# Numerators and weight sums of a plain pair of heads in one 128-row matmul, in the gate stages of a fused attention and GEGLU kernel

## The chip, the cores and the metric

One core of one Trainium2 chip. The metric is the device time of one execution in microseconds (us), the median of several; the executions of one kernel in one comparison lie 0.5 to 2.3 us apart. Ratios are the mean time of one kernel's runs over the mean of the other's runs of the same rounds, so they are not quite the ratio of the medians that are quoted.

## The reference

Attention over 8 batches, 8 heads, 576 positions and 64 dimensions, with a window of 32 keys; heads 0 to 3 ("plain") look at adjacent keys, heads 4 to 7 ("dilated") at every fourth. The heads' outputs, side by side, are 4608 tokens of 512 and go through a GEGLU block.

```python
scores = scale * np.matmul(q, k.transpose(0, 1, 3, 2))
mask_plain = (rel >= 0) & (rel < window)
mask_dil = (rel >= 0) & (rel < window * dilation) & (rel % dilation == 0)
...
attn = np.exp(scores)
attn = attn / (np.sum(attn, axis=-1, keepdims=True) + 1e-09)
out = np.matmul(attn, v)
...
g = x @ w_gate
gelu = 0.5 * g * (1.0 + erf(g * inv_sqrt2))
return gelu * (x @ w_val) @ w_out
```

## The kernel before

It works through 9 chunks of 512 tokens. A chunk has a gate stage (12 units of eight 512-column matmuls: four for the gate, four for the values of the GEGLU, then a gelu on ScalarE and a multiply on VectorE) and an output stage. The attention of later batches is slotted between these matmuls, two heads ("a pair") at a time: 32 pairs, four to a batch, the first two of each batch plain. This study is about seven plain pairs that fall into the gate stages of chunks 3 to 6: 16, 20, 21, 24, 25, 28 and 29.

The kernel's matmuls write to PSUM, which it uses as eight banks of 512 columns. The traces show a weight load for each matmul (2400 of each in the profile before; 98 ns long in the mean for a full one of L481): the operand loaded so is called stationary here. The other one is streamed, and the time goes with its columns: from one start to the next 0.216 us for 512.

For such a pair the kernel computes numerators (probabilities times values) and sums of weights (probabilities times ones), in 64-column tiles: head 0 to PSUM partitions 0 to 63 and head 1 to 64 to 127, at the same columns:

```python
# emit_pv, plain pairs, wide form (cuts marked ...)
for j in range(5):
    for hl in range(2):
        lhs = vp[:, j, 2 * hp + hl, :] if j < 4 else vt[:, 2 * hp + hl, :]
        w = (PW, PW, PW, P, PT)[j]                    # 160, 160, 160, 128, 64
        add(hl, j * P, run(w), lhs, ...)
...
groups = ((0, 0, 4, P), (P, P, 3, 32), (PH - PT, 512, 1, PT))   # 512, 96 and 64 columns
for i, (p0, q0, runs, w) in enumerate(groups):
    for hl in range(2):
        add(hl, d0 + q0, [[P, runs], [1, w]], ones[:, 0:D], ...)
```

VectorE then turns the sums into factors and multiplies. The transpose is used in 18 blocks of 32 columns, to bring the 576 sums, which lie along the columns, onto the partitions; the reciprocal is then taken of 18 columns only, and a second transpose spreads the result (0.78, 0.27 and 0.78 us in the trace before, from 266.04):

```python
# norm_r
nc.vector.transpose(dst, den)                          # 128 x 576, from PSUM
nc.vector.reciprocal(rc, dt[:, :, 0:1]...)             # 128 x 18
nc.vector.transpose(rb..., rc spread by a zero step)   # 128 x 576
# norm_x
nc.vector.tensor_tensor(dst, psf[:, b0 * 512 : b0 * 512 + S], rb, ALU.mult)
```

The gate stage's loop. The pair's four PSUM banks (SB and up) are free for the next pair when its product has been taken; a unit uses one of two pairs of banks in turn:

```python
for nb in range(NNB):                       # 12 units
    ...
    ffn1(c, nb, pairs[(nb + swap) % 2])     # 8 matmuls, then gelu and multiply
    if pend is not None:
        norm_x(pend, SB)
        pend = None
    if nb in pv_at:                         # values_a: chunk -> {unit: pair}
        pend = pv_at[nb]
        emit_pv(pend, SB, wide=True)
        norm_r(pend, SB, wide=True)
```

The softmax here doesn't subtract the row's maximum and nothing guards it: scores larger than these inputs give would overflow.

## Time and profile before

363.44 us, the median of three runs (363.22 to 364.12). The profile's span is 362.5 us, at a granted clock of 0.995.

| engine | busy us | share |
|---|---|---|
| TensorE (PE) | 345.5 | 95% |
| TensorE weight loads (PEld) | 164.2 | 45% |
| VectorE (DVE) | 184.8 | 51% |
| ScalarE (ACT) | 146.0 | 40% |
| GpSimd (POOL) | 78.2 | 22% |

How to read the lines in this document. A group of instructions has line, engine, operation, output <- input and shape, then busy us, the mean ns of one, idle us before it and what ended that idle time. A line of the timeline or of the chain of waits has start us, length us, engine and what ran, with "x8" for eight of it merged. In the chain, a q after an engine's name is its sequencer, and "issue" is time in which the engine waited for nothing that the profile shows. The end of a matmul is modelled, so two matmuls are compared by their starts. L481, L512 and L433 are, before, the gate stage's matmuls, the output stage's, and those of values and sums; after the change the same are L533, L564 and, for the seven changed pairs, L455 (L442 where the old form stays).

### The profile page before, as it was taken

The page shows a single profiled execution, that of the slowest core. Times are in us where ns is not written, and L with a number is a line of the kernel's source. Part 1 is how long each engine was busy: PE and PEld are TensorE (multiplying, and loading weights), DVE is VectorE, ACT ScalarE, POOL GpSimd, SP SyncE. Part 2 cuts the span into 40 slices and gives each one's busy share as a digit, 9 for nine tenths or more (in the row PEclk, how much of TensorE's full clock was granted, in tenths as well). Part 3 has the DMA queues.
Part 4 walks back from the last instruction along what each step waited for, and adds up shares of the span by engine and source line. Part 5 has one row for each costly group of instructions (what it writes and reads, how often), then busy time and mean ns, then how long its engine had stood idle before and what let it go on. Part 6 is the DMA issues. An engine that isn't in the chain of part 4 may idle for free.

```text
span 362.5 us, 6061 instructions
## 1 busy us (share of the span) xinstructions
PE 345.5 (95%) x2400; PEld 164.2 (45%) x2400; DVE 184.8 (51%) x278; ACT 146.0 (40%) x212; POOL 78.2 (22%) x110
## 2 busy tenths in 40 slices
PE   7879899999989999899999999999999999999995
PEld 2554354444544445444444444444444444444442
DVE  1585445744266325864477638783669413303320
ACT  1733255253543345434553356336542223312321
POOL 2580333540432332063003410240000000000000
PEclk9899999999999999999999999999999999999999
DMA  7999999999899898599438962893100030011002
GB/s 184 244 177 214 220 133 194 192 157 235 188 142 204 181 161 154 136 173 135 101 93 186 158 96 89 195 140 72 60 30 2 0 116 2 1 60 58 0 29 89
DMA packets 107292, 45.31 MB, mean 125 GB/s; under 512 B 83040, under 2 KB 102496, under 8 KB 107264
## 3 DMA queue, kind: packets, MB, share of 16 engines
q1 hardware_dynamic: 84272, 31.21, 39.8%
q0 software_dynamic: 21456, 12.01, 26.6%
q10 hardware_dynamic: 1536, 1.70, 2.0%
q8 instruction: 19, 0.31, 0.4%
q14 instruction: 9, 0.07, 0.1%
HBM read 40.13 MB, written 9.44 MB: 137 GB/s over the span
## 4 chain that ended last, share of the span: by engine, by line
PE 78%; DMA 13%; DVE 5%; POOL 2%; ACT 1%; issue 1%; ACTq 0%; SPq 0%; POOLq 0%; DVEq 0%
PE ps L481 41%; PE ps L512 25%; PE ps L433 5%; DMA xT<-in_k_dram 4%; DMA st<-in_k_dram 3%; PE ps L493 3%; DMA wv<-in_moe_w_val_dram 3%; DMA wo<-in_moe_w_out_dram 2%; DVE xT L469 2%; PE ps L360 1%; DMA sv<-in_v_dram 1%; PE ps L330 1%; DVE dt L451 1%; DVE rb L455 1%; PE ps L346 1%; POOL qp L251 1%
## 5 line engine op out<-in xcount | busy, mean ns | idle before, releaser
L506 DVE SCALAR_TENSOR_TENSOR u_all<-g,ps 128x512 f16<-128x512 f16 x108 | 73.5, 686 | 85.9 <-PE ps L481 76.9
L505 ACT ACTIVATE g<-ps 128x512 f16<-128x512 f32 x108 | 63.6, 597 | 126.0 <-PE ps L481 115.0
L512 PE MATMUL ps<-wo,u_all 128*128 128x512 f16 x432 | 101.1, 380 | 1.1 <-DMA wo<-in_moe_w_out_dram 0.7
L481 PE MATMUL ps<-xT,wg 128*128 128x512 f16 x392 | 100.7, 379 | 0.3
L481 PE MATMUL ps<-xT,wv 128*128 128x512 f16 x392 | 100.6, 379 | 0.0
L512 PEld LDWEIGHTS <-u_all 128*128 128x128 f16 x432 | 39.2, 98 | 45.4 <-issue 1.5
L481 PEld LDWEIGHTS <-wv 128*128 128x128 f16 x392 | 38.4, 98 | 46.4 <-issue 0.2
L481 PEld LDWEIGHTS <-wg 128*128 128x128 f16 x392 | 37.2, 98 | 45.0 <-issue 2.1
L523 ACT ACTIVATE osb<-ps 128x512 f32<-128x512 f32 x33 | 19.7, 597 | 49.0 <-PE ps L512 49.0
L451 DVE STREAM_TRANSPOSE dt<-ps 128x576 f32<-128x576 f32 x32 | 24.9, 779 | 26.2 <-PE ps L433 25.9
L190 POOL CAST qp<-st 128x2048 f16<-128x2048 f32 x6 | 11.4, 1894 | 99.0 <-DMA st<-in_k_dram 84.8
L455 DVE STREAM_TRANSPOSE rb<-rc 128x576 f32<-128x576 f32 x32 | 24.9, 778 | 1.1
L362 ACT ACTIVATE P<-ps 128x1152 f16<-128x1152 f32 x16 | 18.1, 1130 | 10.8 <-PE ps L360 10.8
L340 ACT ACTIVATE P<-ps 128x960 f16<-128x960 f32 x16 | 15.5, 970 | 10.7 <-PE ps L330 10.6
L469 DVE TENSOR_TENSOR xT<-ps,rb 128x576 f16<-128x576 f32 x16 | 17.9, 1126 | 0.3
L493 PE MATMUL ps<-xT,wg 128*128 128x512 f16 x40 | 15.2, 379 | 2.1 <-DVE xT L469 1.6
L525 DVE TENSOR_SCALAR osb<-ps 128x512 f32<-128x512 f32 x3 | 2.1, 691 | 28.8 <-PE ps L512 28.8
L433 PE MATMUL ps<-P,ones 128*64 128x96 f16 (+5 forms) x216 | 14.3, 245 | 1.6 <-ACT P L362 1.6
L493 PE MATMUL ps<-xT,wv 128*128 128x512 f16 x40 | 15.2, 379 | 0.0
L466 DVE TENSOR_TENSOR xT<-ps,rb 128x576 f16<-128x576 f32 x16 | 11.8, 745 | 0.3
L370 DVE TENSOR_TENSOR P<-P,mask_p 128x1344 f16<-128x1344 f16 x10 | 8.4, 852 | 6.8 <-ACT P L341 6.8
L370 DVE TENSOR_TENSOR P<-P,mask_d 128x1152 f16<-128x1152 f16 x8 | 6.1, 757 | 11.1 <-ACT P L362 11.1
(75 smaller groups left out, 244.2 us busy)
## 6 DMA issues: line engine op xcount, KB each, us to landing
out_dram<-osb SPq DMA_DIRECT2D x36, 256.0 KB, 2.1
sv<-in_v_dram SPq DMA_DIRECT2D x40, 128.0 KB, 3.2
st<-in_q_dram SPq DMA_DIRECT2D x24, 128.0 KB, 3.7
st<-in_k_dram SPq DMA_DIRECT2D x24, 128.0 KB, 3.1
qd<-in_q_dram POOLq DMA_DIRECT2D x7, 256.0 KB, 5.0
qd<-in_k_dram POOLq DMA_DIRECT2D x7, 256.0 KB, 6.9
vd<-in_v_dram POOLq DMA_DIRECT2D x7, 256.0 KB, 7.2
wg<-in_moe_w_gate_dram POOLq DMA_DIRECT2D x3, 512.0 KB, 7.4
```

Of the source, the lines that this page charges most:

```text
L340: nc.scalar.activation(pt[:, :, 0:PB], sb[:, 0, :, 0:PB], AF.Exp, bias=0.0, scale=scale)
L362: nc.scalar.activation(pt, ps[:, b0 : b0 + 4, 0:DW], AF.Exp, bias=0.0, scale=scale)
L433: nc.tensor.matmul(o, lhs, rhs, start=st, stop=True, skip_group_check=True)
L451: nc.vector.transpose(dst, den)
L455: nc.vector.transpose(rb.rearrange("p (b c) -> p b c", c=32), bass.AP(tensor=rc.tensor, offset=rc.offset, ap=[rc.ap[0], [1, 18], [0, 32]]),)
L469: nc.vector.tensor_tensor(dst.rearrange("p (i m s) -> p i m s", m=2, s=2), num, rb.rearrange("p (s m i) -> p i m s", s=2, m=2), ALU.mult,)
L481: nc.tensor.matmul(ps[:, b0 + gi, :], w[:, kc, ns], xT[kc][:, tok], start=(kc == 0), stop=(kc == NKC - 1))
L493: nc.tensor.matmul(ps[:, pairs[nb] + gi, :], w[:, kc, ns], xT[kc][:, tok], start=(kc == 0), stop=(kc == NKC - 1),)
L505: nc.scalar.activation(g, ps[:, b0, :], AF.Gelu)
L506: nc.vector.scalar_tensor_tensor(u_all[:, nb, :], g, USCALE, ps[:, b0 + 1, :], ALU.mult, ALU.mult)
L512: nc.tensor.matmul(ps[:, bank, :], u_all[:, fc, tb * P : (tb + 1) * P], wo_t[fc // 4][:, fc % 4, :], start=(fc == 0), stop=(fc == NNB - 1),)
L523: nc.scalar.activation(osb, ps[:, bank, :], AF.Copy, bias=0.0, scale=1.0 / USCALE)
```

## The change

The intent: put a head's values next to a block of ones in the stationary operand, so that one matmul of 128 columns gives the numerators of the head in 64 PSUM rows and its sums in the other 64. For the second head of a pair the same block of ones serves from the other side (values, ones, values), so its rows are swapped. The ten matmuls of a pair replace sixteen. Since numerators and sums of the two heads no longer share columns, VectorE needs two transposes and two products of 64 partitions each. The values get permanent tiles with the ones set at the start, the casts into them are strided, and the pairs of chunks 4 to 6 move to other units.

```diff
+    vset = [
+        (
+            const.tile([P, 4, HP, 3, D], F16, tag=f"vp{i}", name=f"vp{i}"),
...
+        nc.gpsimd.tensor_copy(
+            vp.rearrange("p j g x d -> p (j g) x d")[:, :, 0:3:2, :],
+            sv[:, 0:4].rearrange("p j (g x) d -> p (j g) x d", x=2),
+        )
...
+    def emit_both(n, b0):
...
+        for hl in range(2):
+            for j in range(5):
+                w = (PW, PW, PW, P, PT)[j]
+                p0 = j * PW - (32 if j == 4 else 0)
+                trio = vp[:, j, hp] if j < 4 else vt[:, hp]
+                nc.tensor.matmul(
+                    ps[:, b0 + 2 * hl + j // 4, j % 4 * P : j % 4 * P + w],
+                    trio[:, hl : hl + 2, :].rearrange("p x d -> p (x d)"),
+                    pt[:, hl, p0 : p0 + w],
+                    start=j in (0, 4),
+                    stop=True,
+                    skip_group_check=True,
+                )
+
+    def both_rows(half, b0, hl):
+        return psf[64 * half : 64 * half + 64, (b0 + 2 * hl) * 512 : (b0 + 2 * hl) * 512 + S]
+
+    def norm_both_r(n, b0):
+        dt = nrm.tile([P, 18, 32], F32, tag="dt", bufs=1)
+        for hl in range(2):
+            nc.vector.transpose(
+                dt[64 * hl : 64 * hl + 64].rearrange("p b c -> p (b c)"), both_rows(1 - hl, b0, hl)
+            )
+        recip(n, dt)
+
+    def norm_both_x(n, b0):
+        b, hp = divmod(n, NHP)
+        rb = tiles.pop(("rb", n))
+        for hl in range(2):
+            half = slice(64 * hl, 64 * hl + 64)
+            nc.vector.tensor_tensor(
+                xT[hp][half, b * S : (b + 1) * S], both_rows(hl, b0, hl), rb[half], ALU.mult
+            )
...
+    for vp_, _, vt_, _ in vset:
+        nc.vector.memset(vp_.rearrange("p j g x d -> p (j g) x d")[:, :, 1, :], 1.0)
+        nc.vector.memset(vt_[:, :, 1, :], 1.0)
...
-    values_a = {3: {4: 16}, 4: {3: 20, 6: 21}, 5: {2: 24, 4: 25, 6: 26}, 6: {1: 28, 3: 29, 5: 30, 7: 31}}
+    values_a = {3: {4: 16}, 4: {2: 20, 6: 21}, 5: {1: 24, 4: 25, 7: 26}, 6: {1: 28, 4: 29, 7: 30, 10: 31}}
...
-                norm_x(pend, SB)
+                (norm_both_x if is_plain(pend) else norm_x)(pend, SB)
...
+                if is_plain(pend):
+                    emit_both(pend, SB)
+                    norm_both_r(pend, SB)
+                else:
+                    emit_pv(pend, SB, wide=True)
+                    norm_r(pend, SB, wide=True)
```

More of the change, by code (lines that the diff above doesn't have):

```diff
@@ L80 @@
     ldp = ctx.enter_context(tc.tile_pool(name="ldp", bufs=1))
-    vpl = ctx.enter_context(tc.tile_pool(name="vpl", bufs=3))
     qtp = ctx.enter_context(tc.tile_pool(name="qtp", bufs=2))
@@ L100 @@
     xT = [const.tile([P, NT], F16, tag=f"xT{i}", name=f"xT{i}") for i in range(NKC)]
+    HP = HK // 2
+    vset = [
+        (
+            const.tile([P, 4, HP, 3, D], F16, tag=f"vp{i}", name=f"vp{i}"),
+            const.tile([P, HK, 4, D], F16, tag=f"vd{i}", name=f"vd{i}"),
+            const.tile([P, HP, 3, D], F16, tag=f"vt{i}", name=f"vt{i}"),
+            const.tile([P, HK, 2, D], F16, tag=f"vr{i}", name=f"vr{i}"),
+        )
+        for i in range(3)
+    ]
     u_all = const.tile([P, NNB, CH], F16, tag="u")
@@ L160, in new_v @@
     def new_v(b):
-        vp = vpl.tile([P, 4, HK, D], F16, tag="vp", name=f"vp{b}")
-        vd = vpl.tile([P, HK, 4, D], F16, tag="vd", name=f"vd{b}")
-        vt = vpl.tile([P, HK, D], F16, tag="vt", name=f"vt{b}")
-        vr = vpl.tile([P, HK, 2, D], F16, tag="vr", name=f"vr{b}")
         sv = ldp.tile([P, 5, HK, D], F32, tag="sv", name=f"sv{b}")
-        tiles["v", b] = (vp, vd, vt, vr)
+        tiles["v", b] = vset[b % 3]
         return sv
@@ L176, in v_cast @@
         vp, vd, vt, vr = tiles["v", b]
-        nc.gpsimd.tensor_copy(vp, sv[:, 0:4])
-        nc.gpsimd.tensor_copy(vt, sv[:, 4])
+        nc.gpsimd.tensor_copy(
+            vp.rearrange("p j g x d -> p (j g) x d")[:, :, 0:3:2, :],
+            sv[:, 0:4].rearrange("p j (g x) d -> p (j g) x d", x=2),
+        )
+        nc.gpsimd.tensor_copy(vt[:, :, 0:3:2, :], sv[:, 4].rearrange("p (g x) d -> p g x d", x=2))
     def load_qk_plain(b):
@@ L395, in emit_pv @@
                     for hl in range(2):
-                        lhs = vp[:, j, 2 * hp + hl, :] if j < 4 else vt[:, 2 * hp + hl, :]
+                        lhs = vp[:, j, hp, 2 * hl, :] if j < 4 else vt[:, hp, 2 * hl, :]
                         w = (PW, PW, PW, P, PT)[j]
@@ L433, in emit_pv @@
             nc.tensor.matmul(o, lhs, rhs, start=st, stop=True, skip_group_check=True)
+    def emit_both(n, b0):
+        b, hp = n // NHP, n % 2
+        pt = tiles["P", n]
+        vp, _, vt, _ = tiles["v", b]
+        for hl in range(2):
[27 more added lines that the diff above has]
+                xT[hp][half, b * S : (b + 1) * S], both_rows(hl, b0, hl), rb[half], ALU.mult
+            )
     def den_ap(n, b0, wide):
@@ L451, in norm_r, with recip @@
         nc.vector.transpose(dst, den)
+        recip(n, dt)
+    def recip(n, dt):
         rc = nrm.tile([P, 18], F32, tag="rc")
@@ L660 @@
                 pend = pv_at[nb]
-                emit_pv(pend, SB, wide=True)
-                norm_r(pend, SB, wide=True)
+                if is_plain(pend):
[4 more added lines that the diff above has]
+                    norm_r(pend, SB, wide=True)
             if c == 0 and nb in (9, 10):
```

## The prediction

> **What bounds the kernel now**
>
> I read, in this order, the page's summary and slices, its table of groups, the chain that ended last, and then the timeline of TensorE and of VectorE inside the stages that the change touches.
>
> The page first:
>
> ```profile
> span 362.5 us, 6061 instructions
> PE 345.5 (95%) x2400; PEld 164.2 (45%) x2400; DVE 184.8 (51%) x278; ACT 146.0 (40%) x212; POOL 78.2 (22%) x110
> PE 78%; DMA 13%; DVE 5%; POOL 2%; ACT 1%; issue 1%; ACTq 0%; SPq 0%; POOLq 0%; DVEq 0%
> L451 DVE STREAM_TRANSPOSE dt<-ps 128x576 f32<-128x576 f32 x32 | 24.9, 779 | 26.2 <-PE ps L433 25.9
> L466 DVE TENSOR_TENSOR xT<-ps,rb 128x576 f16<-128x576 f32 x16 | 11.8, 745 | 0.3
> ```
>
> TensorE (PE) is busy for 95% and the chain is 78% PE; from about 54 us on, the chain is PE nearly without a break. So the end moves by what PE issues, plus PE's rare waits. VectorE (DVE) averages 51%, but an average hides what it does inside one gate stage. The two DVE rows are the instructions that the change doubles for seven pairs.
>
> The gate stages concerned are chunks 3 to 6. In the chain of waits, chunk 6 (L481: gate and value matmuls; L433: values and sums of one pair):
>
> ```profile
> 260.98 0.86 PE ps L512 x4
> 261.84 3.45 PE ps L481 x16
> 265.29 0.70 PE ps L433 x16
> 266.00 3.56 PE ps L481 x16
> 269.55 0.70 PE ps L433 x16
> 270.26 3.57 PE ps L481 x16
> ...
> 278.25 0.72 PE ps L433 x12
> 278.97 7.01 PE ps L481 x32
> 285.98 10.36 PE ps L512 x48
> ```
>
> Each plain pair is a bite of PE time between two units of eight 512-column matmuls. In a later stage without pairs the chain has 96 such matmuls in 20.72 us: 0.216 us each, 1.727 us a unit. Chunks 3, 4, 5 and 6 last 18.24, 19.16, 23.20 and 24.14 us.
>
> What a bite really costs is in the PE timeline at the pair of chunk 3:
>
> ```profile
> 158.41 0.38 PE L481 MATMUL ps<-xT,wv 128*128 128x512 f16 x1
> 158.72 0.45 PE L433 MATMUL ps<-P,vp 128*64 128x160 f16 x8
> 159.01 0.20 PE L433 MATMUL ps<-P,vt 128*64 128x64 f16 x2
> 159.04 0.46 PE L433 MATMUL ps<-P,ones 128*64 128x512 f16 x6
> 159.43 0.61 PE L481 MATMUL ps<-xT,wg 128*128 128x512 f16 x2
> ```
>
> The last 512-column matmul starts at 158.41; the next start would be due 0.216 later, at 158.63, but is at 158.72: 0.09 lost on entering 64-column tiles. The next gate matmul starts at 159.43. So the bite is 159.43 - 158.63 = 0.80 us. The 16 matmuls run in pairs, two heads side by side, so they stream 672 columns of values and 672 of ones, 1344 column times in all.
>
> DVE's time of chunk 6:
>
> ```profile
> 266.04 0.78 DVE L451 STREAM_TRANSPOSE dt<-ps 128x576 f32<-128x576 f32 x1
> 266.85 0.27 DVE L453 RECIPROCAL rc<-dt 128x18 f32<-128x18 f32 x1
> 267.15 0.78 DVE L455 STREAM_TRANSPOSE rb<-rc 128x576 f32<-128x576 f32 x1
> 267.94 0.69 DVE L506 SCALAR_TENSOR_TENSOR u_all<-g,ps 128x512 f16<-128x512 f16 x1
> 268.54 0.75 DVE L466 TENSOR_TENSOR xT<-ps,rb 128x576 f16<-128x576 f32 x1
> ```
>
> Start to start a pair takes about 0.82 + 0.30 + 0.78 + 0.75 = 2.65 us of DVE, plus 0.6 to 0.69 for each unit's multiply. With a pair every two units (before) that is 3.9 us against 2 x 1.727 + 0.80 = 4.25 us of PE: DVE is nearly full here. Yet PE waits only twice in chunk 6: 0.06 us at 273.80 and 0.24 at 278.25.
>
> [...] 12 transposes of 128 columns take 0.84 us from first start to last end, each 0.22 long, so (0.84 - 0.22)/11 = 0.056 us apart. The weight load of 128 columns keeps up at that size.
> [...]
>
> **The change part by part**
>
> *PE, per plain pair in a gate stage.* Six matmuls over ones vanish (42 in all), ten of 64 columns become ten of 128, unpaired. Two heads x (3 of 160, one of 128, one of 64 columns) is again 1344 column times: the streaming is not reduced. What goes is the mode switch in and out and the starting cost. At 0.069, 0.056 and 0.029 us the new bite is 2 x (3 x 0.069 + 0.056 + 0.029) = 0.584 us. The old one is 0.80, plus 0.01 since the second gap after it is 0.227 and not 0.216. Saved: 0.81 - 0.585 = 0.22 us; seven pairs (16, 20, 21, 24, 25, 28, 29) make 1.55 us. All on PE, so on the path.
>
> *DVE, per such pair.* One transpose of the sums becomes two over 64 partitions, one product becomes two. Time follows the 576 columns, not the partitions, so I take 0.78 and 0.745 again for each half: +1.52 us[...]. Seven pairs: +10.7 us busy, off the path unless PE waits.
>
> *DVE at the start.* Six memsets: 3 x (0.48 + 0.15) = 2 us, right after the memset of ones at 0.9 us. DVE then idles 6.9 us for data, so nothing is lost.
>
> *POOL.* The value casts write strided runs of 64. 1024 elements now take 1.04 to 1.13 us (one contended one 1.60); a cast already in runs of 64 takes 0.82 for 768, the same rate. The first cast (18.84) lies on the startup chain, so 0.1 us more would be 0.1 us of the end. I take 0.
>
> *The places moved.* Pairs in chunks 5 and 6 stand three units apart instead of two. Does DVE keep up? A period is three units and a bite on PE, 3 x 1.727 + 0.585 = 5.77 us, against DVE: transposes 0.70 + 0.81 to the reciprocal, 0.82, 0.30, then 0.78 for the spread, products 1.55, and three multiplies (about 0.70, 0.61, 0.64, partly in those steps): near 6.1 us. DVE is over PE by some 0.3 us. Only consecutive pairs show it.
>
> Walk of chunk 6, t = 0 where unit 1 ends on PE: bite to 0.59. Multiply(1) from 0.27; transposes 0.97 and 1.78; reciprocal 2.60; spread 2.90; multiply(2) 3.68; products 4.29 and 5.06, ended at 5.80; multiply(3) 5.84. Unit 4 ends at 5.78; its value half starts at 4.91 and needs multiply(2), ended at 4.37: no wait. Pair 29 must wait for the product: 5.86 instead of 5.78, 0.08 lost. From there multiply(4) 6.46, transposes 7.16 and 7.97, reciprocal 8.79, spread 9.09, multiply(5) 9.87, products 10.48 and 11.25, ended at 12.0. Unit 7's value half at 10.77 needs multiply(5), ended at 10.56: it just fits. Pair 30 (dilated, old form) would start at 11.73 and starts at 12.05: 0.32 lost. Pair 31 finds DVE caught up. So PE waits 0.40 us where it waited 0.30.
>
> Chunk 5 begins 0.17 us behind on DVE (the first gelus wait for a table load), so pair 25 loses 0.25 and pair 26 0.33, where the old kernel lost nothing. Chunks 3 and 4 have four units or more between pairs and lose nothing, with only 0.06 us to spare at one value half.
>
> Sum, by stage: chunk 3 -0.22; chunk 4 -0.44; chunk 5 -0.44 + 0.58 = +0.14; chunk 6 -0.44 + 0.10 = -0.34. Together **-0.86 us**: 363.44 becomes 362.6. I write 362.7, leaving 0.1 for the startup casts.
>
> **Rivals**
>
> *A. All of the PE saving arrives* [...]: -1.5 us, 361.9. For it: the spacing was widened, probably until the waits were gone. Against: a period's sum is 6.1 against 5.77 us.
>
> *B. DVE becomes the bound of chunks 5 and 6*, [...] value halves waiting for multiplies in chunks 3 and 4 too: 0.3 us more per pair gives -0.86 + 7 x 0.3 = +1.2 us, 364.7. For it: margins of 0.06 to 0.15 us. Against: chunk 4 has slack of a whole unit.
>
> *C. Streaming is really halved*, the plain reading of "one matmul instead of two": 0.28 us less per pair, -3 us. Against: the old matmuls already run two heads side by side; their starts come in pairs[...].
>
> *D. The startup shifts* with POOL's strided casts or the memsets: up to +0.5 us by the transfers of weights behind them. The idle time before the first data speaks against the memsets.
>
> None reaches 2%, which is 7.3 us.
>
> **Range and chances**
>
> The runs before span 363.22 to 364.12, so 0.5 us is noise. A gives 361.9 and half of B 363.7: I take 361.8 to 363.8. Within 2%: 0.98; 0.01 each for faster and slower.
>
> **What would show each step right or wrong**
>
> - PE timeline at a plain pair: ten matmuls 128*128, a bite near 0.59 us and starts 0.216 us after the last 512-column one. A bite of 0.45 or less would make C right[...].
> - DVE groups: 14 transposes and 14 products of 64x576, at 780 and 745 ns; half of that would bring A.
> - Chain of waits in chunks 5 and 6: pieces of DVE before the second and third pair, 0.1 to 0.3 us each; chunk lengths near 18.0, 18.7, 23.3 and 23.8 us.
> - DVE busy near 197 us in all, the six memsets ended before the first cast.
> - The first value cast still about 1.04 us long, and chunk 0's second half at the same time (54.4 us).

An addition to DVE's time of a pair for starts that are delayed, which no trace had shown, is in the steps of the walk, which takes 0.70 us from a multiply to the transpose after it where the trace before has 0.60 (270.01 to 270.62; the trace after has 0.72), and so in the waits of 0.58 and 0.40 us; what it takes above the 0.60 was not shown when it was written. The other figures of the steps can be read in the profile before:

- Streams: the matmuls of the two heads start 0.003 to 0.004 us apart, and after such a pair of 160, 128 and 64 columns the next starts 0.069, 0.056 and 0.028 us later (from 158.81).
- The switch and the starting cost, alike within 0.002 us in all seven places: 0.309 us instead of 0.216 on entering, 0.094 instead of 0.069 for the first pair of streams, 0.128 instead of 0.029 on leaving, and 0.227 instead of 0.216 after the first gate matmul.
- The 12 transposes are L281's, from 15.00: after the second their weight loads, 98 ns long, start 0.055 to 0.058 us apart, and the matmuls themselves 0.055 to 0.056.
- Rival C: at 0.216 us for 512 columns, 1344 columns are 0.567 us of the 0.80, an estimate; half of that is its 0.28.
- Memsets: that of ones, 512 elements, took 0.48 us at 0.92; the 0.15 for 128 elements was my estimate (0.17 in the trace after).
- Table load: 1.28 us on ScalarE at 225.92, in chunk 5; the first gelu starts right after it, at 227.22.

## The result, and the profile after

362.44 us, the median of four runs (361.88 to 362.64), against 363.78 us (363.22 to 364.22) for the kernel before in the same rounds: ratio 0.9962, 95% interval 0.9941 to 0.9982. In a longer comparison, below, it is 0.9955. The change is worth some 1.4 to 1.6 us: a small gain.

The page of the kernel after: the summary and the chain.

```profile
span 359.8 us, 5997 instructions
PE 344.5 (96%) x2358; PEld 166.2 (46%) x2358; DVE 196.0 (54%) x298; ACT 145.9 (41%) x212; POOL 78.2 (22%) x110
PE 88%; DVE 5%; DMA 3%; ACT 1%; issue 1%; ACTq 0%
```

PE has 42 matmuls fewer and still sets the end. DVE is busier by 11.2 us. The chain's share of DMA fell from 13% to 3%, which says little of the time: in the profile before, the chain ran through the transfers of keys, values and weights of the first 54 us, with PE waiting 0.7 us for the last of them; in this one another path through the same stretch came out longest. What the startup is worth is taken up in the last part of the experiments.

DVE's two new groups, with shapes kept apart:

```profile
L470 DVE STREAM_TRANSPOSE dt<-ps 64x576 f32<-64x576 f32 x14 | 10.9, 781 | 0.4
L480 DVE TENSOR_TENSOR xT<-ps,rb 64x576 f16<-64x576 f32 x14 | 10.5, 748 | 0.2
```

Half the partitions take the same time: 781 ns against 779 for 128 partitions, 748 against 745. So the change pays 7 x (0.781 + 0.748) = 10.7 us of DVE.

PE's timeline at the pair of chunk 3:

```profile
157.05 0.81 PE L533 MATMUL ps<-xT,wv 128*128 128x512 f16 x3
157.70 0.43 PE L455 MATMUL ps<-P,vp 128*128 128x160 f16 x4
157.96 0.19 PE L455 MATMUL ps<-P,vt 128*128 128x64 f16 x1
157.99 0.43 PE L455 MATMUL ps<-P,vp 128*128 128x160 f16 x4
158.25 0.19 PE L455 MATMUL ps<-P,vt 128*128 128x64 f16 x1
158.28 1.03 PE L533 MATMUL ps<-xT,wg 128*128 128x512 f16 x4
```

The three matmuls from 157.05 start 0.216 apart, the last at 157.48, and the pair begins 0.216 us after that: nothing is lost on entering. It ends where the next gate matmul starts: 158.28 - 157.70 = 0.58 us, or 0.584 by the unrounded starts, in each of the seven places (0.583 in one). Before, it was 0.80.

The chain of waits, in order of time: pair 26 of chunk 5, then chunk 6.

```profile
238.10 0.75 PE ps L442 x16
...
259.88 3.45 PE ps L533 x16
263.33 0.59 PE ps L455 x10
263.92 5.18 PE ps L533 x24
269.10 0.59 PE ps L455 x10
269.68 5.18 PE ps L533 x24
274.86 0.65 PE ps L442 x16
275.52 5.29 PE ps L533 x24
```

There is no DVE in chunk 6's chain any more. The only wait left in these stages is inside pair 26: 0.75 where a dilated pair takes 0.65 (by starts, 0.846 against 0.748 us). It is the pair's sums that wait, the matmuls into its last two banks.

DVE's timeline there:

```profile
264.16 1.59 DVE L470 STREAM_TRANSPOSE dt<-ps 64x576 f32<-64x576 f32 x2
265.79 0.27 DVE L505 RECIPROCAL rc<-dt 128x18 f32<-128x18 f32 x1
266.09 0.78 DVE L507 STREAM_TRANSPOSE rb<-rc 128x576 f32<-128x576 f32 x1
266.79 0.65 DVE L558 SCALAR_TENSOR_TENSOR u_all<-g,ps 128x512 f16<-128x512 f16 x1
267.36 1.53 DVE L480 TENSOR_TENSOR xT<-ps,rb 64x576 f16<-64x576 f32 x2
...
270.24 1.59 DVE L470 STREAM_TRANSPOSE dt<-ps 64x576 f32<-64x576 f32 x2
```

A period of DVE is 270.24 - 264.16 = 6.08 us with no gap in it, longer than PE's 5.77 (269.10 - 263.33). So DVE falls 0.3 us behind in each, as predicted, and yet PE does not wait.

Where the time came from, by stage. I measure a stage by PE's starts, from its first unit (chunks 5 and 6) or its third (chunks 3 and 4) to the first matmul after it. The last row is the kernel of the last experiment.

| | chunk 3 | chunk 4 | chunk 5 | chunk 6 | sum | time ratio |
|---|---|---|---|---|---|---|
| before | 18.17 | 19.10 | 23.20 | 24.15 | 84.62 | 1 |
| after | 17.94 | 18.65 | 22.85 | 23.41 | 82.85 | 0.9962; 0.9955 |
| places only | 18.17 | 19.10 | 23.20 | 23.86 | 84.33 | 0.9996 |
| layout only | 18.17 | 19.10 | 23.21 | 23.86 | 84.34 | 0.9985 |
| switch added | 18.20 | 19.16 | 23.27 | 23.92 | 84.55 | 0.9999 |
| products swapped | 17.94 | 18.65 | 23.22 | 23.72 | 83.53 | 0.9959 |
| VectorE single | 17.94 | 18.65 | 22.75 | 23.41 | 82.75 | 0.995 |
| old places | 17.94 | 18.81 | 25.55 | 26.44 | 88.74 | 1.012 |
| pair 26 later | 17.94 | 18.65 | 23.07 | 23.41 | 83.07 | 0.9956 |
| pair 25 later | 17.94 | 18.65 | 22.76 | 23.41 | 82.76 | 0.9946 |

The rest of the program does not change: from the end of chunk 6's gate stage to the end of the program every profile has 76.66 to 76.68 us. These stage lengths repeat to 0.01 us, where the whole time scatters by half a microsecond and more.

### The profile page after: what moved, and what is told of

Its sections match the earlier page's. It is cut to its first block, busy times and chain, and to the rows that moved or that the text cites. A ratio compares the mean times of both kernels' runs of the same rounds, so it can differ in the third digit from the quotient of the medians. Undisturbed runs are those within 1.5% of the kernel's fastest.

```text
span 359.8 us, 5997 instructions
## 1 busy us (share of the span) xinstructions
PE 344.5 (96%) x2358; PEld 166.2 (46%) x2358; DVE 196.0 (54%) x298; ACT 145.9 (41%) x212; POOL 78.2 (22%) x110
## 4 chain that ended last, share of the span: by engine, by line
PE 88%; DVE 5%; DMA 3%; ACT 1%; issue 1%; ACTq 0%
PE ps L533 47%; PE ps L564 26%; PE ps L442 5%; PE ps L545 4%; DMA xT<-in_k_dram 3%; PE ps L369 2%; PE ps L339 1%; DVE dt L500 1%; DVE rb L507 1%; DVE xT L521 1%; PE ps L355 1%; PE ps L455 1%; PE ps L332 1%; ACT P L371 1%; DVE rc L505 0%
## 5 line engine op out<-in xcount | busy, mean ns | idle before, releaser
L558 DVE SCALAR_TENSOR_TENSOR u_all<-g,ps 128x512 f16<-128x512 f16 x108 | 72.6, 683 | 75.8 <-PE ps L533 65.7
L500 DVE STREAM_TRANSPOSE dt<-ps 128x576 f32<-128x576 f32 x25 | 19.5, 779 | 25.7 <-PE ps L442 25.6
L521 DVE TENSOR_TENSOR xT<-ps,rb 128x576 f16<-128x576 f32 x16 | 17.8, 1124 | 0.3
L442 PE MATMUL ps<-P,ones 128*64 128x192 f16 (+5 forms) x174 | 11.6, 248 | 2.0 <-ACT P L371 1.0
L470 DVE STREAM_TRANSPOSE dt<-ps 64x576 f32<-64x576 f32 x14 | 10.9, 781 | 0.4
```

Of the source, the lines that this page charges most:

```text
L442: nc.tensor.matmul(o, lhs, rhs, start=st, stop=True, skip_group_check=True)
L521: nc.vector.tensor_tensor(dst.rearrange("p (i m s) -> p i m s", m=2, s=2), num, rb.rearrange("p (s m i) -> p i m s", s=2, m=2), ALU.mult,)
L558: nc.vector.scalar_tensor_tensor(u_all[:, nb, :], g, USCALE, ps[:, b0 + 1, :], ALU.mult, ALU.mult)
```

## The experiments

My theory: the gain is PE's, and it is the switch of tiling around each pair, not the streaming and not the wider spacing; DVE's doubling costs nearly nothing since the next pair waits for only one of the two products. The rivals: the places did it; fewer instructions did it; DVE has slack.

### The changed kernel again

No edit.

> The changed kernel again, to narrow its gain. Chunks 3, 4, 5 and 6 should last 18.0, 18.7, 22.9 and 23.4 us as in its first profile (before: 18.24, 19.16, 23.20, 24.14; sum of the gain 1.74 us). If the stages are all there is, the time is 1.7 us under before, ratio 0.9952; if the startup gives something back, 1.0 to 1.4 us, ratio 0.996 to 0.997.

Measured: 362.00 us (361.63 to 363.03, six runs) against 363.95 (362.79 to 364.33, eleven runs); ratio 0.9955, interval 0.9940 to 0.9969; stages 17.94, 18.65, 22.85 and 23.41 us. 0.0045 x 363.95 is 1.6 us, the stages give 84.62 - 82.85 = 1.77 us. So the stages account for the gain; the smaller 1.4 us of the first four runs lies within their scatter.

### The places alone

```diff
 # the kernel before
-    values_a = {3: {4: 16}, 4: {3: 20, 6: 21}, 5: {2: 24, 4: 25, 6: 26}, 6: {1: 28, 3: 29, 5: 30, 7: 31}}
+    values_a = {3: {4: 16}, 4: {2: 20, 6: 21}, 5: {1: 24, 4: 25, 7: 26}, 6: {1: 28, 4: 29, 7: 30, 10: 31}}
```

> The kernel before with the changed kernel's places of the pairs, nothing else. Theory 1 (the gain is TensorE time at each pair): only the two waits of chunk 6 (0.06 + 0.24 us) go; chunk 6 from 24.14 to 23.85 us, the others unchanged, ratio 0.999. Theory 2 (the gain is mainly the wider spacing): chunks 5 and 6 fall to near 22.9 and 23.4, ratio 0.996.

Measured: 363.84 us, ratio 0.9996 (0.9976 to 1.0016). Chunk 5 stays at 23.20 us, chunk 6 falls to 23.86: just the two waits of 0.06 and 0.24 us. The spacing by itself is worth 0.29 us.

### The layout alone

```diff
 # the changed kernel
-                (norm_both_x if is_plain(pend) else norm_x)(pend, SB)
+                norm_x(pend, SB)
...
-                if is_plain(pend):
-                    emit_both(pend, SB)
-                    norm_both_r(pend, SB)
-                else:
-                    emit_pv(pend, SB, wide=True)
-                    norm_r(pend, SB, wide=True)
+                emit_pv(pend, SB, wide=True)
+                norm_r(pend, SB, wide=True)
```

> The changed kernel with its memsets, strided casts, permanent value tiles and places, but the pairs in the old 64-column form. If the layout is free: as places_only, ratio 0.999, startup the same within its own scatter. If the memsets or strided casts cost startup time: 0.3 to 0.5 us more than places_only.

Measured: 363.37 us, ratio 0.9985 (0.9971 to 0.9998); the stages are those of the places alone. The two intervals overlap, so a difference of layout is not shown in either direction; a cost of 0.3 to 0.5 us would have put this kernel above the one with the places alone, and its mean is 0.5 us below. In the trace the six memsets run from 1.46 to 3.45 us, before DVE's first data at 7.66, and the first strided cast takes 1.04 us as the dense one did.

### The switch put back

```diff
 # the changed kernel, at the end of emit_both
+        for half in range(2):
+            nc.tensor.matmul(
+                ps[64 * half : 64 * half + 64, b0 + 1, 256:320],
+                ones[:, 0:D],
+                pt[:, half, 0:64],
+                start=True, stop=True, skip_group_check=True,
+            )
```

> The changed kernel with two extra 64-column matmuls of 64 columns (side by side, into an unused stretch) at the end of each of the seven pairs: 0.029 us of streaming, and a switch of tiling into and out of it. Theory 1 (what was saved is the switch): the pair's bite grows from 0.584 to about 0.80 us, seven pairs give back 1.5 us, time within 0.3 us of before, ratio 0.999. Theory 2 (what was saved is the number of matmuls and weight loads, 16 to 10): the bite grows by 0.03 to 0.06 us, ratio stays near 0.996.

Measured: 364.02 us, ratio 0.9999 (0.9985 to 1.0012): the whole gain is gone. The bite is 0.831 us in each of the seven places. PE's timeline at chunk 3 (in this kernel L464 is the added pair and L542 the gate stage):

```profile
158.89 0.19 PE L455 MATMUL ps<-P,vt 128*128 128x64 f16 x1
159.01 0.22 PE L464 MATMUL ps<-P,ones 128*64 128x64 f16 x2
159.17 0.61 PE L542 MATMUL ps<-xT,wg 128*128 128x512 f16 x2
```

From the last 64-column-wide stream at 158.89 to the added pair is 0.12 us where a matmul of 64 columns is otherwise followed after 0.029; from the added pair to the gate matmul is 0.15. Of 0.831 - 0.584 = 0.247 us, 0.029 are streaming, 0.22 are the switch in and out. That is the whole of what the change saves at a pair, 0.81 - 0.584. The rival of fewer instructions is out: this kernel has only four matmuls fewer than before at each pair, and two more than the changed one. What within the switch takes the time stays open. In the steady streams a weight load starts with the matmul before its own (in the trace after, at 157.48 for the matmul at 157.70); at a switch it starts only together with its own (in the trace before, at 158.72 on entering and at 159.42 on leaving, for matmuls at 158.72 and 159.43). No run here tells whether the late weights are its cause.

### The two products in the other order

```diff
 # the changed kernel, in norm_both_x
-        for hl in range(2):
+        for hl in (1, 0):
```

> The changed kernel with the two products of a pair in the other order (head 1's half first). Theory 1 (the next pair waits only for the product that reads the banks it writes first, so it starts while the second product still runs): now the product that it needs first comes last, so PE waits of 0.1 to 0.3 us appear before pairs 25, 26 and 30; chunk 5 from 22.86 to about 23.15 us, chunk 6 from 23.41 to about 23.65. Theory 2 (it waits for both products anyway, DVE is simply in time): no change, 22.86 and 23.41.

Measured: 362.26 us, ratio 0.9959 (0.9928 to 0.9989, too wide to tell it from the changed kernel); chunk 5 23.22 us, chunk 6 23.72, so 0.37 and 0.31 us more than after. PE's starts show waits of 0.27 us before pair 25, 0.20 before 26, 0.11 before 29 and 0.20 before 30. The chain of waits at pair 25:

```profile
231.33 0.76 DVE xT L480
232.09 0.01 issue
232.10 0.76 DVE xT L480
232.86 0.04 issue
232.91 0.47 PE ps L455 x5
```

Here PE starts 0.05 us after the end of the second product. In the changed kernel pair 25 starts at 232.17, while the two products there run from 230.76 to 232.29, and pair 30 starts at 274.79, with pair 29's products running until 274.97: each starts before the second product has ended. The only difference is which product comes last. So the release goes by half: the first matmuls of a pair write the first two of its four banks, and need only the product that reads those.

### VectorE's work as before, result wrong on purpose

```diff
 # the changed kernel; dt is one permanent tile, half of it stale
-        for hl in range(2):
-            nc.vector.transpose(dt[64 * hl : 64 * hl + 64]..., both_rows(1 - hl, b0, hl))
+        nc.vector.transpose(dt[0:64].rearrange("p b c -> p (b c)"), both_rows(1, b0, 0))
...
-        for hl in range(2):
-            ...
-            nc.vector.tensor_tensor(xT[hp][half, ...], both_rows(hl, b0, hl), rb[half], ALU.mult)
+        nc.vector.tensor_tensor(
+            xT[hp][:, b * S : (b + 1) * S], psf[:, b0 * 512 : b0 * 512 + S], rb, ALU.mult
+        )
```

> Wrong result on purpose: the changed kernel's matmuls, but one transpose and one product per pair instead of two, so VectorE does as much as before. If the doubling costs what I predicted (0.58 us in chunk 5, 0.40 in chunk 6), those fall to 22.3 and 23.0 us. If it costs only the 0.10 us seen at pair 26, chunk 5 falls to 22.76 and chunk 6 stays at 23.41; the time is the same within 0.1 us.

Measured: 361.60 us, ratio 0.995 (0.9923 to 0.9976); DVE busy 187.0 us instead of 196.0. Chunk 5 22.75 us, chunk 6 23.41. So nine microseconds of DVE less buy 0.10 us of PE: the doubling costs that and no more. (Here nothing reads the two banks of a changed pair's second head, so no wait for these can arise either; the 0.10 includes whatever such waits cost.)

### The old places

```diff
 # the changed kernel
-    values_a = {3: {4: 16}, 4: {2: 20, 6: 21}, 5: {1: 24, 4: 25, 7: 26}, 6: {1: 28, 4: 29, 7: 30, 10: 31}}
+    values_a = {3: {4: 16}, 4: {3: 20, 6: 21}, 5: {2: 24, 4: 25, 6: 26}, 6: {1: 28, 3: 29, 5: 30, 7: 31}}
```

> The changed kernel with the pairs at the old places, two units apart in chunks 5 and 6. VectorE then needs some 5.4 us for each plain pair and two multiplies against 4.04 us of TensorE. Theory 1: waits of about 1.4 us before each pair that follows a plain one (two in chunk 5, two in chunk 6), chunk 5 near 25.6 us, chunk 6 near 26.5, time some 4 us over before, ratio 1.011. Theory 2 (VectorE is not near its limit): under 0.5 us, ratio 0.997.

Measured: 367.76 us (367.36 to 368.62), ratio 1.012 (1.0093 to 1.0147): slower than the kernel before. Chunk 5 25.55 us, chunk 6 26.44, and chunk 4, with three units between its pairs, 0.16 longer than after: there a value half, at 206.06, starts 0.376 us after the matmul before it instead of 0.216, as soon as DVE's late multiply of 205.32 is done (205.32 + 0.69 = 206.01). Two lines of the table of waits, us in total, times, longest:

```profile
PE ps L455 <- DVE xT L480: 2.2, 4, 0.8
PE ps L442 <- DVE xT L480: 2.2, 4, 0.8
```

Each of the four pairs that follow a plain one in chunks 5 and 6 (25 and 29 in the new form, 26 and 30 in the old) waits twice, once for each product: 0.94 us or a little less before its first matmul and some 0.5 us in its middle, 1.4 in all. So the spacing, which gains next to nothing alone, is what makes the change possible.

### Pair 26 one unit later: a miss

```diff
-    5: {1: 24, 4: 25, 7: 26}
+    5: {1: 24, 4: 25, 8: 26}
```

> The changed kernel with pair 26 one unit later (8 instead of 7). The 0.10 us wait inside that pair (its bite 0.846 against 0.748 us) should go: chunk 5 from 22.86 to 22.76 us; the time the same within noise.

Measured: 361.91 us, ratio 0.9956 (0.9932 to 0.9979). The wait at pair 26 went (its bite is 0.747 us), but chunk 5 grew to 23.07 us. The lines of DVE and of PE around unit 8:

```profile
238.21 1.29 DVE L558 SCALAR_TENSOR_TENSOR u_all<-g,ps 128x512 f16<-128x512 f16 x2
```

```profile
238.95 1.02 PE L533 MATMUL ps<-xT,wv 128*128 128x512 f16 x4 [0.15 <-DVE u_all L558]
```

The value half of unit 8 writes the bank that the multiply of unit 6 reads. DVE comes to that multiply only at 238.21, after the products of pair 25; it ends at 238.90 and PE starts at 238.95, 0.32 us after the start that was due (the gate half's four matmuls begin at 237.76 and take 4 x 0.216). With pair 26 after unit 7 its bite had stood in that place and covered the delay. The backlog was real; I had only moved what PE runs into.

### Pair 25 one unit later

```diff
-    5: {1: 24, 4: 25, 7: 26}
+    5: {1: 24, 5: 25, 8: 26}
```

> The changed kernel with chunk 5's pairs after units 1, 5 and 8 instead of 1, 4 and 7. Theory (VectorE falls 0.3 us behind in each period of three units, and the wait at pair 26 is what two such periods pile up; pair 26 one unit later had moved the wait to a value half that needs the multiply of unit 6): four units let VectorE catch up, so neither wait appears; chunk 5 from 22.85 to 22.75 us, pair 26's bite 0.748, ratio 0.995. Rival (any change of places brings a wait somewhere in chunk 5): chunk 5 at 22.85 or above.

Measured: 361.89 us (360.86 to 363.20, six runs) against 364.16 (eleven runs), ratio 0.9946 (0.9929 to 0.9963). Chunk 5 is 22.76 us and pair 26's bite 0.748. Its chain of waits:

```profile
226.23 6.91 PE ps L533 x32
233.14 0.58 PE ps L455 x10
233.73 5.18 PE ps L533 x24
238.91 0.65 PE ps L442 x16
```

With four units after pair 24, DVE catches up and no wait is left in chunks 3 to 6: the same 22.75 as with half of DVE's work taken away. This is the best version. By its stages it is 0.09 us better than the changed kernel, which its times (intervals that overlap) cannot show.

### The startup

The start of chunk 1's gate stage is at 69.03 us in the profile before, 68.94 with the places alone, 68.42 with the layout alone, and between 67.17 and 68.77 in the eight profiles of the new form. Those eight issue the same matmuls up to there and spread over 1.6 us. All nine profiles with the new startup (the layout alone is one) do begin chunk 1 earlier than the two with the old one, and their chains hold 2 to 5% of DMA against 13 and 10%; but the profile before is of a slow execution, 364.59 us, where the medians of that kernel are 363.4 to 364.2. The times settle more: in the nine comparisons of kernels with the new startup, the gain in the mean time is between 0.37 us less and 0.39 us more than the gain of the four stages, and 0.06 more on average. So an effect of the startup is not shown, one of 0.9 us is not what these times have, and the 2.7 us between the two spans must not be read as the gain.

## Why the prediction was right

The time lay in the range, 362.44 (362.00 later) for 362.7, and the mechanism held for PE and for DVE's own times, not for the waits between them. That the time fitted is partly luck: the range of 2 us held nearly everything from no gain to rival A, and the stages gained 1.77 us, twice the 0.86 predicted. Taken apart, the 1.77 are 7 x 0.226 = 1.58 for the bites, 0.29 for the two waits of chunk 6 that the places removed, less 0.10 for the wait inside pair 26. By the prediction's steps:

- **The bite of PE.** Predicted 0.584 us; measured 0.584 in all seven places. Its ten weight loads, 98 ns long in the trace after and starting as little as 0.029 us apart, delayed no matmul: the starts are 0.069, 0.056 and 0.029 us apart, as in the old pairs. The saving, 0.22 us a pair, is the switch, as the run with the switch put back shows.
- **Rival C, halved streaming.** Out: 0.45 us or less would have been needed.
- **DVE per pair.** Predicted 0.78 and 0.745 for each half, a period near 6.1 us; measured 0.781, 0.748 and 6.08.
- **Delayed starts.** The first half transpose starts 0.72 us after the multiply before it (263.44 to 264.16 in the trace), where a full one before that had no PE to wait for started after 0.60 (270.01 to 270.62). The walk had 0.70; no run isolates a cause.
- **The step that was mis-sized: the waits of PE for DVE.** Predicted 0.58 us in chunk 5 and 0.40 in chunk 6, 0.98 together; measured 0.10 and 0. These 0.88 us are nearly all of the 0.91 between the sums of stages, -1.77 and -0.86. The prediction's sentence "Pair 29 must wait for the product: 5.86 instead of 5.78" took the end of both products; a pair's first matmuls need only the first. With the products swapped, where the last one does gate, the waits were 0.27, 0.20, 0.11 and 0.20, for 0.25, 0.33, 0.08 and 0.32 predicted: 0.78 against 0.98. So the walk was nearly right for another kernel. The remainder is DVE again: after the spreading transpose the multiply started 0.70 and not 0.78 us later (266.09 to 266.79), 0.08 a pair.
- **Rival A** ("all of the PE saving arrives", 361.9) is what came, but not because DVE had time to spare: its period is 6.08 us against PE's 5.77. That was hidden by the release in halves and by the few consecutive pairs there are.
- **The startup.** Predicted 0 for the memsets, 0 to 0.1 for the casts: nothing is seen, within a scatter of 1.6 us between profiles. The six memsets took 0.48 us for 512 elements and 0.17 for 128, 1.99 us from the first start to the last end for 2 predicted.

## What to carry to other kernels

Two small matmuls side by side streamed as fast here as one of full width (160 columns every 0.069 us, for the pair as for the one), so the merge into one full-width matmul gained the switch of tiling at the borders, 0.22 us a pair, and not the columns: count switches, not instructions. Before giving a second engine more work per item, compare periods (its work between two items against the bound engine's), space the items by that, and look for the wait that a moved item had been covering. When an item is released in parts, order the parts so that what the next one touches first is freed first.
